# Weight words loaded one pair sooner and five weight conversions moved into the first batch's pairs

## The chip, the cores and the metric

The kernel runs on one core of a Trainium2 chip. The metric is the device time in microseconds (us), as the median of several runs. All times inside an execution are counted from the start of its span.

## The reference: what is computed

Feature-map attention over 8 batches of 8 heads, 576 tokens and head width 64, followed by a mixer over the 512 channels that the heads make together:

```python
def phi(x):
    proj = np.einsum('bhsd,df->bhsf', x, w_phi)
    proj = proj - np.max(np.abs(proj), axis=-1, keepdims=True)
    return np.concatenate([np.exp(proj), np.exp(-proj)], axis=-1)
q_p, k_p = phi(q), phi(k)
kv, z = np.einsum('bhsf,bhsd->bhfd', k_p, v), np.sum(k_p, axis=2)
x = np.einsum('bhsf,bhfd->bhsd', q_p, kv) / (np.einsum('bhsf,bhf->bhs', q_p, z)[..., None] + 1e-06)
# heads side by side: x is (8, 576, 512)
h = x.transpose(0, 2, 1) @ U @ V          # over tokens, rank 32
u = x + h.transpose(0, 2, 1)
out = u + np.maximum(u @ w_ch1, 0.0) @ w_ch2   # 512 -> 2048 -> 512
```

q, k, v and w_phi are float32. U, V and the two channel matrices are float64 and come to the chip as pairs of 32-bit words.

## The kernel before

**Work.** Attention goes in 32 pairs of heads, four to a batch: pair (b, j) is heads 2j and 2j+1 of batch b. For each pair k, q and v are loaded (`Pair`, `load_v`), k and q are transposed, projected (`pk`, `pq`), turned into features (`kp`, `qp`: absolute maxima, a subtraction, two exponentials on ACT, L372/L373 and L384/L385; for `qp` the maximum is an all-reduce on POOL, L382), the keys are summed with v on TensorE (`kv_ps`), and the outputs (`xp`, `xpt`) are divided and put into the token tile `x`. In batches 0 and 1 the transposes go through TensorE and PSUM, later through DVE. When all four pairs of a batch are there, `Tokens` mixes over tokens: `split` makes high and low parts `xs`, `down` multiplies by U into `pp` and then `pst`, `up` multiplies by V (`vp`) and adds. Then a `Mixer` tile transposes 512 tokens (`pt`, `uT_hi`, `uT_lo`) and runs 16 blocks of `hidden` (L651, 12 matmuls into `ph`; then `h_hi` on ACT and `h_lo` on DVE) and `add` (L672, 12 matmuls into four `o` tiles). The 64 last tokens of all batches make a ninth tile at the end.

**Weights.** The channel matrices come in 16 blocks. `load_weights(f)` issues two transfers of 512 KB on SP. `convert_block(i)` turns half a block into float32 parts: three ACT operations (L137, L138, L140), one shift on DVE (L141), an integer addition on POOL (L145), a copy (ACT for w1, DVE for w2, L239) and a subtraction on DVE (L240). There are 32 such conversions, here called blocks too where it is plain. Blocks 0 and 8 are also stored to memory (`kept`, L236) for later batches. Block 15's words use the place of `x0`, the first batch's tokens.

**Order.** A scheduler that plans with costs of its own sets the order on each engine from the order in which the code is traced; on the chip each engine then runs its list in that order. The code traces attention in steps (`step`), and after each step `Pace.step` adds other work: conversions up to a number that grows with the step count `steps[0]` (`blocks`), pieces of the first batch's token work (`pieces`), chunks of the mixer (`mix`), and, while the mixer has no chunks, one matmul over zeros (`keep_busy`), which is pinned in program order. A conversion is held behind the last operations put into `made` (the splits, `pst`, sums and transposed tiles of the first batch):

```python
for ins in made[-1:]:
    for i in ins:
        order.enter_context(tc.issue_after(i.ins))
convert_block(converted[0])
```

The words of blocks up to `LOADS[n]` are loaded at the start of pair number n, and held behind that pair's own loads.

**Names in the order's rows.** `qp0_2_1` is the query feature tile of pair (0,2), second half; `T1_0_3` the transposed q of pair (0,3) (T0 is k); `w1_0_ab` a working tile of the conversion of block 0 of w1; the number behind is a running number.

Of the kernel before, what the change touches and what calls it, by code (L numbers as in the profile page):

```python
# [25 lines left out]
def tile_kernel(  # L26
# [26 lines left out]
    NFC = DFF // P  # L53
# [135 lines left out]
    LAST = NFC - 1  # L189
# [523 lines left out]
    def weights(upto):  # L713

        while loaded[0] <= min(upto, LAST):
            load_weights(loaded[0])
            loaded[0] += 1
# [23 lines left out]
    steps = [0]  # L741

    class Pace:
# [5 lines left out]
        def step(self):  # L749

            steps[0] += 1
            upto = (steps[0] - CONVERT[0]) * 2 * NFC // (CONVERT[1] - CONVERT[0])
            if not pieces:
                blocks(upto)
            else:
                pieces.pop(0)()
                blocks(upto)
                if not pieces:
                    self.chunks, self.steps = 32 - HELD, BATCH - steps[0]
                else:  # L760
                    keep_busy(1, True)
                return
            n = (self.at + 1) * self.chunks // self.steps - self.at * self.chunks // self.steps
            self.at += 1
            mix(n)
            if not self.chunks:

                keep_busy(1, True)

# [9 lines left out]
            if here:  # L779
                tc.keep_in_program_order(ins)  # L780

    LOADS = (-1, 1, 4, 8, 12, LAST)
    CONVERT = (28, 63)
    BATCH = 67
    pieces = []
    HELD = 4
# [57 lines left out]
    def first_tokens(tk):  # L844
        m = []

        def begin():
            tk.up(2)
            tk.up(3)
            m.append(Mixer(tk.b, tk.x))  # L850
            m[0].transposes(0)

        def end():
            m[0].transposes(3)
            todo.extend(m[0].chunks())

        return [
            lambda: tk.split(1),
            lambda: [tk.down(1)] + [tk.up(t) for t in range(2)],
            lambda: [begin(), m[0].transposes(1), tk.up(NT)],  # L860
            lambda: [m[0].transposes(2), end()]]

    if True:
        cur = Pair(0, 0)
        load_w_phi()
        cur.load_v()
        nxt = Pair(0, 1)
        load_uv()
        nxt.load_v()
        keep_busy(6)  # L870
        cur.transposes()
        cur.s_project_k0()
        cur.s_project_k1()
        cur.s_project_q0()
        nxt.transposes()
        cur.s_kv()
        cur.s_project_q1()
        x = home.tile([P, NT, C], F32, tag="w_last", name="x0")
        xt = moe.tile([P, C], F32, tag="xt", name="xt0")
        nc.vector.memset(xt[ST:P], 0.0)  # L880
        tk = Tokens(0, x, xt)
        for n, (b, j) in enumerate(pairs):

            far = Pair(*pairs[n + 2]) if n + 2 < len(pairs) else None
            if far is not None:
                far.load_v()
            if n < len(LOADS):

                with tc.issue_after(far.loaded.ins):
                    weights(LOADS[n])  # L890
            if nxt is not None:
                step(nxt.s_project_k0)
            step(cur.s_out, x, xt)
            if nxt is not None:
                step(nxt.s_project_k1)
            pace.step()
            if j == 1:
                tk.split(0)
            if j == NPAIR - 1:
                fill = []  # L900
                if nxt is not None:
                    fill = [far.transposes, nxt.s_project_q0, nxt.s_kv, nxt.s_project_q1]
                if b == 0:
                    pieces.extend(first_tokens(tk))
                    pieces.pop(0)()
                    for fn in fill:
                        step(fn)
                else:
                    tokens(tk, fill)
                    pace = Pace(32 - HELD, 34)  # L910
                if nxt is not None:
                    if b % 2 == 1:
                        xt = moe.tile([P, C], F32, tag="xt", name=f"xt{b + 1}")
                        nc.vector.memset(xt[ST:P], 0.0)
                    x = moe.tile([P, NT, C], F32, tag="x", name=f"x{b + 1}")
                    tk = Tokens(b + 1, x, xt)
            else:
                if n == 0:
                    convert_uv()
                if far is not None:  # L920
                    step(far.transposes)
                if j == 1:
                    step(tk.down, 0)
                step(nxt.s_project_q0)
                step(nxt.s_kv)
                step(nxt.s_project_q1)
            cur, nxt = nxt, far
        mix(len(todo) - HELD)
        x = moe.tile([P, NT, C], F32, tag="x", name="x_tail")
        nc.sync.dma_start(out=x, in_=u_rows(B))  # L930
        m = Mixer(B, x)
        m.load_blocks()
        for c in range(NCC):
            m.turn_blocks(c)
            mix()
        todo.extend(m.chunks())
        mix(len(todo))
# [31 lines left out]
```

## Time and profile before

| | |
|---|---|
| median of 3 runs | 1175.15 us (1172.83 to 1176.64) |
| the profiled execution | 1178.5 us, span 1176.7 us |
| granted TensorE clock, mean | 0.989 |
| busy PE / DVE / ACT / POOL | 1133.4 / 671.2 / 542.1 / 204.3 us |
| matmuls over zeros | 37 |
| matmul groups of the mixer (L651 and L672) | 3456 matmuls of 128x512 |

PE is TensorE's matmuls, PEld its weight loads, DVE VectorE, ACT ScalarE, POOL GpSimd, SP the engine that issues the transfers. A timeline row gives start, length, engine, line, operation, tile written and tiles read, how many were merged, and in brackets the idle time ahead and what ended it. Lengths of neighbouring rows overlap a little, so the distance between two starts is the better price of one operation.

### The profile page before, as it was taken

What the parts mean: (1) busy time and instruction counts of PE and PEld (TensorE: products, weight loads), DVE (VectorE), ACT (ScalarE), POOL (GpSimd) and SP (SyncE); (2) the same over time, 40 slices, a digit from 0 to 9 for tenths busy, and PEclk for the clock granted to TensorE, in tenths of its full rate; (3) what the DMA queues carried; (4) which work ended last, traced back from release to release, by engine and by line L of the source; (5) the groups of instructions that cost most, each with busy time, mean ns of one, the idle gap of its engine ahead of it and who ended that gap; (6) DMA issues with size and microseconds to landing.
All of it is one profiled execution on the core that took longest, in us unless ns stands there. A gap on an engine that the chain in (4) does not pass through costs nothing.

```text
span 1176.7 us, 22653 instructions
## 1 busy us (share of the span) xinstructions
PE 1133.4 (96%) x8845; PEld 928.1 (79%) x8845; DVE 671.2 (57%) x1482; ACT 542.1 (46%) x1151; POOL 204.3 (17%) x154
## 2 busy tenths in 40 slices
PE   8998999999999999999999999999999999999998
PEld 6767877778877787778787887788777887888886
DVE  5567888766666656765656566765666543312111
ACT  6678887545443544454434554454544431111110
POOL 3334455211111111011111111111101110000000
PEclk8999999999999999999999999999999999999999
DMA  5775321431334223441344124522344026310101
GB/s 148 229 232 209 113 58 32 113 95 32 71 101 105 49 59 85 85 104 31 85 106 117 28 55 115 109 55 53 82 96 103 1 72 157 99 36 6 67 1 36
DMA packets 248427, 100.89 MB, mean 86 GB/s; under 512 B 215424, under 2 KB 227968, under 8 KB 248320
## 3 DMA queue, kind: packets, MB, share of 16 engines
q1 hardware_dynamic: 248000, 98.92, 32.8%
q8 instruction: 70, 1.15, 0.4%
q10 hardware_dynamic: 320, 0.52, 0.1%
q14 instruction: 37, 0.30, 0.1%
HBM read 78.41 MB, written 20.97 MB: 84 GB/s over the span
## 4 chain that ended last, share of the span: by engine, by line
PE 67%; DVE 11%; SPq 8%; DMA 7%; ACT 3%; issue 2%; POOL 1%; DVEq 0%; ACTq 0%; POOLq 0%
PE o L672 25%; PE ph L651 25%; SPq L279 5%; PE kv_ps L464 4%; PE xp L508 3%; SPq L637 2%; DMA raw<-in_k_dram 2%; DMA raw<-in_q_dram 2%; DVE T L338 2%; PE pp L587 2%; DVE raw L334 1%; PE pk L403 1%; PE pk L418 1%; DVE w L240 1%; PE kv_ps L455 1%
## 5 line engine op out<-in xcount | busy, mean ns | idle before, releaser
L651 PE MATMUL ph<-uT_hi,w 128*128 128x512 f32 x1152 | 387.2, 398 | 8.2 <-DVE den_t L478 3.6
L672 PE MATMUL o<-w,h_hi 128*128 128x512 f32 x1152 | 326.7, 398 | 7.5 <-ACT h_hi L656 7.5
L651 PEld LDWEIGHTS ph<-uT_hi,w 128*128 128x128 f32 x1152 | 217.5, 189 | 60.0 <-DVE h_lo L657 6.3
L672 PEld LDWEIGHTS o<-w,h_hi 128*128 128x128 f32 x1152 | 211.4, 189 | 52.3 <-ACT h_hi L656 12.1
L651 PE MATMUL ph<-uT_lo,w 128*128 128x512 f32 x576 | 227.0, 394 | 2.4 <-DVE uT_lo L249 2.4
L656 ACT ACTIVATE h_hi<-ph 128x512 fp32r<-128x512 f32 x144 | 85.6, 595 | 265.0 <-PE ph L651 253.6
L657 DVE SCALAR_TENSOR_TENSOR h_lo<-ph,h_hi 128x512 fp32r<-128x512 f32 x144 | 98.9, 687 | 170.9 <-ACT h_hi L656 170.0
L672 PE MATMUL o<-w,h_lo 128*128 128x512 f32 x576 | 192.7, 397 | 0.9 <-DVE h_lo L657 0.9
L382 POOL PARTITION_ALL_REDUCE qp<-qp x64 | 128.8, 2014 | 307.7 <-ACT qp L381 307.3
L651 PEld LDWEIGHTS ph<-uT_lo,w 128*128 128x128 f32 x576 | 109.4, 190 | 24.5 <-DVE uT_lo L249 2.9
L672 PEld LDWEIGHTS o<-w,h_lo 128*128 128x128 f32 x576 | 105.4, 188 | 22.1 <-DVE h_lo L657 2.1
L382 POOL PARTITION_ALL_REDUCE qp_t<-qp_t x32 | 26.2, 820 | 368.3 <-ACT qp_t L381 368.3
L334 DVE STREAM_TRANSPOSE raw<-raw 128x512 f32<-128x512 f32 x48 | 34.1, 711 | 92.5 <-DMA raw<-in_k_dram 39.4
L337 ACT CAST T<-raw 64x512 fp32r<-64x512 f32 x96 | 59.4, 618 | 51.0 <-PE pq L442 48.8
L372 ACT ACTIVATE kp<-kp 128x512 f32<-128x512 f32 x64 | 40.4, 631 | 92.0 <-DVE kp L369 91.9
L508 PEld LDWEIGHTS xp<-kv,qp 128*64 128x64 f32 x2048 | 66.4, 139 | 16.3 <-issue 7.8
L508 PE MATMUL xp<-kv,qp 128*64 128x65 f32 x2048 | 73.5, 226 | 5.3 <-ACT qp L384 4.0
L338 DVE TENSOR_TENSOR T<-raw,T 64x512 fp32r<-64x512 f32 x96 | 68.0, 708 | 17.6 <-ACT T L337 15.1
L464 PE MATMUL kv_ps<-vb,kp 128*64 128x65 f32 x2048 | 71.2, 224 | 0.0
L464 PEld LDWEIGHTS kv_ps<-vb,kp 128*64 128x64 f32 x2048 | 64.2, 137 | 8.6 <-issue 3.8
L384 ACT ACTIVATE qp<-qp 128x512 f32<-128x512 f32 x64 | 40.4, 631 | 65.8 <-DVE qp L383 65.8
L421 ACT COPY kp<-pk 128x256 f32<-128x256 f32 x96 | 34.0, 370 | 44.6 <-PE pk L418 43.7
(125 smaller groups left out, 1328.2 us busy)
## 6 DMA issues: line engine op xcount, KB each, us to landing
words<-in_moe_w_ch_dram SPq DMA_DIRECT2D x32, 512.0 KB, 7.2
w<-kept SPq DMA_DIRECT2D x30, 512.0 KB, 4.7
vb<-in_v_dram SPq DMA_DIRECT2D x64, 128.0 KB, 3.1
u_dram<-x SPq DMA_DIRECT2D x32, 256.0 KB, 2.1
st<-u_dram SPq DMA_DIRECT2D x16, 512.0 KB, 4.6
out_dram<-st SPq DMA_DIRECT2D x32, 256.0 KB, 2.5
y<-u_dram SPq DMA_DIRECT2D x112, 64.0 KB, 2.4
raw<-in_k_dram SPq DMA_DIRECT2D x192, 32.0 KB, 2.0
```

The costliest lines, as they stand in the source:

```text
L279: self.loaded = nc.sync.dma_start(out=m[i * Q:(i + 1) * Q, g, :].rearrange("c (j r) -> c j r", r=Q), in_=src[b, self.h0 + g, rs, cs].rearr ...
L334: nc.vector.transpose(out=x_, in_=x_)
L337: nc.scalar.copy(out=m[here, s, :], in_=x_[here])
L338: nc.vector.tensor_sub(m[there, s, :], x_[here], f32(m[here, s, :]))
L372: nc.scalar.activation(out=kp[:, :, 0:F], in_=kp[:, :, F:2 * F], func=AF.Exp)
L382: nc.gpsimd.partition_all_reduce(qp[:, 0, :], qp[:, 1, :], P, ReduceOp.absmax)
L464: nc.tensor.matmul(self.kv_v[r_, f, g, :], kp[:, t, f * F + i * H:f * F + (i + 1) * H], self.vb[:, g, t, :], start=False, stop=(t == NT - ...
L508: nc.tensor.matmul(xv[i * H:(i + 1) * H, c, :], qp[:, f, c * P + i * H:c * P + (i + 1) * H], self.kv[:, f, c // 2 if self.split else s, :] ...
L651: nc.tensor.matmul(ph, w1_part(f, l, c), r[:, c, :], start=(n == 0), stop=(n == 3 * NCC - 1))
L656: on_act = nc.scalar.activation(out=h_hi, in_=ph, func=AF.Relu)
L657: on_dve = nc.vector.scalar_tensor_tensor(out=h_lo, in0=ph, scalar=0.0, in1=f32(h_hi), op0=ALU.max, op1=ALU.subtract)
L672: ins = nc.tensor.matmul(self.o[t], l[:, cs], w2_t[f][:, r, :], start=(f == 0 and n == 0), stop=(f == NFC - 1 and n == 2))
```

## The change

Four edits. (1) `LOADS` loses its first entry, so that blocks 0 and 1 are loaded with pair 0 and each later group one pair sooner. (2) Conversions: before, the count was (step - 28) * 32 // 35, so the first came at step 30. Now it is (min(step, 26) - 10) * 5 // 16 up to step 30, which traces one at each of steps 14, 17, 20, 23 and 26, and 5 + (step - 31) * 27 // 32 from step 31, which gives the sixth at step 33. Both end at step 63. Steps 9 to 25 are those of pairs 1 and 2. (3) `Pace.step` leaves out its matmul over zeros at steps 8 to 22; in pair 0 three are added ahead of and three behind the outputs. (4) Two empty pieces follow the first batch's token work, so that the mixer's chunks begin two steps later: the first `hidden` is traced at step 36 for 34, behind the outputs of pair (1,0) instead of ahead of them.

```diff
@@ Pace.step
-            upto = (steps[0] - CONVERT[0]) * 2 * NFC // (CONVERT[1] - CONVERT[0])
+            if steps[0] < CONVERT[0]:
+                upto = (min(steps[0], EARLY[1]) - EARLY[0]) * EARLY[2] // (EARLY[1] - EARLY[0])
+            else:
+                upto = EARLY[2] + (steps[0] - CONVERT[0]) * (2 * NFC - EARLY[2]) // (
+                    CONVERT[1] - CONVERT[0])
...
-            if not self.chunks:
+            if not self.chunks and not 7 < steps[0] < 23:
 
                 keep_busy(1, True)
@@
-    LOADS = (-1, 1, 4, 8, 12, LAST)
-    CONVERT = (28, 63)
+    LOADS = (1, 4, 8, 12, LAST)
+    EARLY, CONVERT = (10, 26, 5), (31, 63)
@@ first_tokens
-            lambda: [m[0].transposes(2), end()]]
+            lambda: [m[0].transposes(2), end()],
+            lambda: None, lambda: None]
@@ the loop over pairs
+            if n == 0:
+                keep_busy(3, True)
             step(cur.s_out, x, xt)
+            if n == 0:
+                keep_busy(3, True)
```

What the scheduler makes of it, at three places. **First place: the end of batch 0's first token half, pairs 2 and 3.** ACT before, from the copy of the first `pst`:

```order
L590 CAST pst0_671<-pp0_0_672 128x256
L347 COPY T1_0_3_667<-T1_0_3_662 128x512
L381 COPY qp0_2_1_740<-pq1_0_2_737 128x512
L372 ACTIVATE kp0_3_t_773<-kp0_3_t_773 128x128
L373 ACTIVATE kp0_3_t_773<-kp0_3_t_773 128x128
L384 ACTIVATE qp0_2_0_690<-qp0_2_0_690 128x512
L381 COPY qp0_3_t_858<-pqt0_3_856 128x128
L385 ACTIVATE qp0_2_0_690<-qp0_2_0_690 128x512
```

ACT now, from the same copy of `pst` on; the rows go on in the next fence with the last of the twelve:

```order
L590 CAST pst0_679<-pp0_0_680 128x256
L137 ACTIVATE w1_0_ab_693<-words0_1_307 128x512
L138 ACTIVATE w1_0_ab_693<-words0_1_307 128x512
L140 ACTIVATE w1_0_ab_693<-words0_1_307 128x512
L137 ACTIVATE w2_0_ab_758<-words0_2_308 128x512
L138 ACTIVATE w2_0_ab_758<-words0_2_308 128x512
L140 ACTIVATE w2_0_ab_758<-words0_2_308 128x512
L137 ACTIVATE w1_1_ab_883<-words1_1_311 128x512
L138 ACTIVATE w1_1_ab_883<-words1_1_311 128x512
L140 ACTIVATE w1_1_ab_883<-words1_1_311 128x512
L137 ACTIVATE w2_1_ab_921<-words1_2_312 128x512
L138 ACTIVATE w2_1_ab_921<-words1_2_312 128x512
```

Four conversions stand between `pst` and the T1 copy of pair (0,3). ACT now, further on:

```order
L140 ACTIVATE w2_1_ab_921<-words1_2_312 128x512
L347 COPY T1_0_3_677<-T1_0_3_672 128x512
L381 COPY qp0_2_1_752<-pq1_0_2_749 128x512
L372 ACTIVATE kp0_3_t_796<-kp0_3_t_796 128x128
L381 COPY qp0_3_t_877<-pqt0_3_875 128x128
L239 CAST w1_0_699<-w1_0_ab_693 128x512
L357 COPY tail_T1_0_894<-tT1_0_892 64x2x64 x2
L384 ACTIVATE qp0_2_0_706<-qp0_2_0_706 128x512
L372 ACTIVATE kp0_3_0_805<-kp0_3_0_805 128x4x128
L239 CAST w1_1_889<-w1_1_ab_883 128x512
L137 ACTIVATE w1_2_ab_1026<-words2_1_545 128x512
```

Behind the last row come two more operations of that conversion, an exponential of `kp0_3_t`, and then the second exponential of `qp0_2_0` (L385). TensorE there, before:

```order
L446 MATMUL pq1_0_2_737<-T1_0_2_457,w_two_89 128x2x128 x2
L395 MATMUL pkt0_3_771<-w_f_87,tail_T0_3_651 128x128
L403 MATMUL pk0_0_3_779<-w_two_89,T0_0_3_658 128x256 x2
L778 LDWEIGHTS zeros_115
L778 MATMUL busy_685<-zeros_115 128x512
L433 MATMUL pqt0_3_856<-tail_T0_3_651,w_f_87 128x128
L493 MATMUL xpt0_2_790<-kv0_2_733,qp0_2_t_626 64x65 x4
L324 MATMUL tT1_0_868<-ident_82,t_r1_0_752 128x128
L342 MATMUL T0_1_0_872<-ident_82,raw1_0_0_748 128x128 x4
L778 LDWEIGHTS zeros_115
L778 MATMUL busy_696<-zeros_115 128x512
L508 MATMUL xp0_0_2_803<-kv0_2_733,qp0_2_0_690 64x65 x2
```

and now:

```order
L493 MATMUL xpt0_2_811<-kv0_2_747,qp0_2_t_640 64x65 x4
L433 MATMUL pqt0_3_875<-tail_T0_3_661,w_f_87 128x128
L324 MATMUL tT1_0_892<-ident_82,t_r1_0_772 128x128
L342 MATMUL T0_1_0_896<-ident_82,raw1_0_0_768 128x128 x4
L342 MATMUL T1_1_0_905<-ident_82,raw1_0_1_770 128x128 x4
L446 MATMUL pq0_0_3_912<-T1_0_3_677,w_two_89 128x2x128 x2
L782 LDWEIGHTS zeros_115
L782 MATMUL busy_930<-zeros_115 128x512
L508 MATMUL xp0_0_2_824<-kv0_2_747,qp0_2_0_706 64x65 x16
L508 MATMUL xp1_0_2_845<-kv0_2_747,qp0_2_1_752 64x65 x2
L403 MATMUL pk1_0_3_866<-w_two_89,T0_0_3_668 128x256 x2
```

The transposes of pair (1,0) and the projection of q of pair (0,3) now all stand ahead of the outputs of pair (0,2), and two zeros between them are gone.

**Second place: the second token half and the first mixer tile.** ACT before:

```order
L137 ACTIVATE w1_0_ab_1128<-words0_1_531 128x512
L138 ACTIVATE w1_0_ab_1128<-words0_1_531 128x512
L140 ACTIVATE w1_0_ab_1128<-words0_1_531 128x512
L381 COPY qp1_0_0_1143<-pq0_1_0_1140 128x512
L137 ACTIVATE w2_0_ab_1177<-words0_2_532 128x512
L138 ACTIVATE w2_0_ab_1177<-words0_2_532 128x512
L140 ACTIVATE w2_0_ab_1177<-words0_2_532 128x512
L590 CAST pst0_671<-pp0_1_1107 128x256
```

ACT now, from the split to the first transposed tile:

```order
L248 CAST xs0_1_4_1125<-xt0_296 128x256
L381 COPY qp1_0_0_1174<-pq0_1_0_1171 128x512
L590 CAST pst0_679<-pp0_1_1148 128x256
L248 CAST uT_hi0_1188<-pt0_0_1190 128x4x128
L384 ACTIVATE qp1_0_0_1174<-qp1_0_0_1174 128x512
L347 COPY T1_1_1_1146<-T1_1_1_1141 128x512
L381 COPY qp1_0_1_1266<-pq1_1_0_1263 128x512
```

The two conversions ahead of `pst` are gone. Behind the last `uT_hi` copy and two operations of block 2 of w2, ACT now goes on so (before, six conversion operations stood there, of blocks w1_1 and w2_1):

```order
L140 ACTIVATE w2_2_ab_1272<-words2_2_546 128x512
L137 ACTIVATE w1_3_ab_1323<-words3_1_549 128x512
L138 ACTIVATE w1_3_ab_1323<-words3_1_549 128x512
L372 ACTIVATE kp1_1_t_1308<-kp1_1_t_1308 128x128
L140 ACTIVATE w1_3_ab_1323<-words3_1_549 128x512
L137 ACTIVATE w2_3_ab_1387<-words3_2_550 128x512
L138 ACTIVATE w2_3_ab_1387<-words3_2_550 128x512
L140 ACTIVATE w2_3_ab_1387<-words3_2_550 128x512
L372 ACTIVATE kp1_1_0_1317<-kp1_1_0_1317 128x4x128
L373 ACTIVATE kp1_1_t_1308<-kp1_1_t_1308 128x128
L384 ACTIVATE qp1_0_1_1266<-qp1_0_1_1266 128x512
L656 ACTIVATE h_hi0_0_1409<-ph0_0_1396 128x512
```

Nine conversion operations are now ahead of the exponential of `qp1_0_1`.

**Third place: SP's queue ahead of pair (1,1).** Before:

```order
L217 DMA words4_2_768<-in_moe_w_ch2_dram 128x1024
L307 DMA vb0_91<-in_v_dram 128x4x64
L296 DMA t_r1_1_955<-in_k_dram 64x2x64
L285 DMA raw1_1_0_951<-in_k_dram 128x2x256
L296 DMA t_r1_1_955<-in_q_dram 64x2x64
L285 DMA raw1_1_1_953<-in_q_dram 128x2x256
```

and now:

```order
L214 DMA words8_791<-in_moe_w_ch1_dram 128x4x256
L217 DMA words8_791<-in_moe_w_ch2_dram 128x1024
L296 DMA t_r1_1_986<-in_k_dram 64x2x64
L296 DMA t_r1_1_986<-in_q_dram 64x2x64
L236 DMA kept0_104<-w2_0_764 128x1024
L285 DMA raw1_1_0_982<-in_k_dram 128x2x256
L236 DMA kept0_104<-w1_0_699 128x1024
L285 DMA raw1_1_1_984<-in_q_dram 128x2x256
```

The words of four more blocks and the two stores of block 0 now stand ahead of that pair's raw tiles.

## Prediction

> **What bounds the kernel now.** I read the page first, then busy time in windows cut at the stages, then the rows of each engine at the places where the order changes.
>
> ```profile
> span 1176.7 us, 22653 instructions
> ...
> PE 1133.4 (96%) x8845; PEld 928.1 (79%) x8845; DVE 671.2 (57%) x1482; ACT 542.1 (46%) x1151; POOL 204.3 (17%) x154
> ```
>
> ```profile
> 16.00:30.00 14.00, 11.18 (x124) 8.43 (x123) 12.26 (x40) 9.40 (x24) 7.12 (x7) 0.77 0.54 147
> ...
> 54.00:66.00 12.00, 11.91 (x159) 9.04 (x158) 5.78 (x18) 7.14 (x16) 5.08 (x5) 1.00 0.69 220
> ...
> 76.00:92.00 16.00, 11.93 (x153) 9.56 (x151) 11.76 (x25) 12.62 (x25) 6.58 (x4) 0.99 0.71 225
> ...
> 108.00:160.00 52.00, 52.00 (x412) 43.27 (x411) 39.49 (x72) 44.37 (x87) 28.09 (x21) 1.00 0.38 109
> 160.00:180.00 20.00, 17.37 (x129) 13.09 (x128) 17.73 (x37) 17.23 (x32) 6.82 (x5) 0.91 0.06 10
> 180.00:245.00 65.00, 60.00 (x503) 48.25 (x502) 51.96 (x106) 40.47 (x84) 20.05 (x13) 0.97 0.29 79
> 245.00:1000.00 755.00, 736.45 (x6056) 608.02 (x6055) 457.23 (x1035) 345.33 (x754) 109.44 (x69) 1.00 0.34 79
> ```
>
> The columns are the stretch, its length, busy PE, PEld, DVE, ACT and POOL, the granted TensorE clock, the DMA share and GB/s. From 245 on TensorE is busy 736.45 of 755 us and its work is fixed, so nothing changed earlier is absorbed there: the end moves by as much as the state at 245 moves. Everything the diff touches lies ahead of 245, and there TensorE loses time in few places: 2.8 of 14 us in the first pairs, 4.1 of 16 from 76 on, 2.6 of 20 from 160 on and 5.0 of 65 after that, plus half clock where the last but two columns fall under 1.00. I follow one number through the program: how much later (+) or earlier (-) than before the changed kernel is at a given instruction.
>
> **Matmuls over zeros.** 37 become 30: fifteen steps lose theirs, six are added in the first pair, two come with the empty pieces.
>
> ```profile
> L778 PE MATMUL busy<-zeros x37: 376/389/634, 1.2 to 85.6; 128*128 128x512 bf16 x37
> ...
> 49.02 0.39 PE L778 MATMUL busy<-zeros 128*128 128x512 bf16 x1
> 49.34 0.56 PE L464 MATMUL kv_ps<-vb,kp 128*64 128x65 f32 x10
> ```
>
> One costs the next matmul 0.32 us (49.02 to 49.34). By the order, up to the second transposes of pair 3 both kernels have nine of them behind 28 us, so the six new ones and those left out cancel: 0. The dip of the clock near 24 us (0.50 below) has its cause in a wait for an exponential, which stays; its bounds are -3.4 (it is gone: 6.8 us at half) and +1.3 (three zeros at half clock on the path), and I take -0.5, near nothing. From there to the last q projection of pair 2 three are gone, three times 0.32: -0.9, and the first pst copy, which two of them and a few matmuls of kv_ps precede, comes near 48.0.
>
> **The twelve conversion operations on ACT.** This is the step that decides. Five blocks are traced earlier, but all are held behind the first pst copy, and the order puts four of them, twelve ACT operations, in one piece right behind it, ahead of T1 of pair 3.
>
> ```profile
> 48.85 0.37 ACT L590 CAST pst<-pp 128x256 fp32r<-128x256 f32 x1 [1.83 <-PE pp L587]
> 51.00 0.59 ACT L347 COPY T<-T 128x512 f32<-128x512 f32 x1 [1.77 <-PE pq L446]
> 51.48 0.59 ACT L381 COPY qp<-pq 128x512 f32<-128x512 f32 x1
> ...
> 52.53 0.61 ACT L384 ACTIVATE qp<-qp 128x512 f32<-128x512 f32 x1
> ...
> 53.19 0.63 ACT L385 ACTIVATE qp<-qp 128x512 f32<-128x512 f32 x1
> ...
> 89.16 0.79 ACT L137 ACTIVATE w_ab<-words 128x512 uint16<-128x512 uint16 x1
> ...
> 92.77 0.63 ACT L372 ACTIVATE kp<-kp 128x512 f32<-128x512 f32 x1
> ```
>
> ```profile
> 54.78 1.04 PE L508 MATMUL xp<-kv,qp 128*64 128x65 f32 x28
> ...
> 57.73 1.13 PE L403 MATMUL pk<-w_two,T 128*128 128x256 f32 x4
> ...
> 72.71 1.04 PE L508 MATMUL xp<-kv,qp 128*64 128x65 f32 x28 [0.90 <-ACT qp L385]
> ```
>
> Six such operations ran from 89.16 to 92.77, 0.60 us each, so twelve hold ACT 7.2 us where it idled 1.77. With pst at 48.0 and 0.4 long they end at 55.6: the T1 copy is 4.6 late. Behind it stand a copy, an exponential, a copy, a cast and two short copies (2.6 us) before the first exponential of qp0_2_0, at 58.2 for 52.53; then an exponential, a cast, three more conversion operations and a short one (3.2 us, and the exponential's own 0.6) before the second, at 62.0 for 53.19. TensorE has work until about 52; its next transposes need the PSUM tile that the late qp copy frees, about 57, and the outputs of pair 2 need both exponentials. So it idles near 52 to 57 and near 60 to 62.6, outputs come at 62.6, and after 1.04 for them and 0.3 for two of the next half, pk (57.73 before) runs at 64.0: +6.3. Two fewer zeros until the next pair's keys: +5.7. DVE and POOL carry their parts of these blocks beside this wait, at no cost as long as ACT is the later one. Bounds: +2 (only the T1 copy counts) and +8.8 (the second exponential's delay in full).
>
> **What comes back before the mixer.** At the outputs of pair 3 the two exponentials now stand together, so the 0.90 wait at 72.71 goes, with one zero 0.3: +4.5.
>
> ```profile
> 76.02 1.41 PE L587 MATMUL pp<-xs,u_all 128*128 128x256 f32 x9
> ...
> 80.32 0.37 ACT L590 CAST pst<-pp 128x256 fp32r<-128x256 f32 x1
> ...
> 83.68 0.43 DVE L141 TENSOR_SCALAR w_ab<-w_ab 128x512 int32<-128x512 int32 x1
> ...
> 86.99 0.87 DVE L141 TENSOR_SCALAR w_ab<-w_ab 128x512 int32<-128x512 int32 x1
> ...
> 89.64 0.67 DVE L240 TENSOR_TENSOR w<-w_ab,w 128x512 fp32r<-128x512 f32 x1
> ```
>
> Before, six conversion operations kept the second pst copy until 80.32 though its matmuls ended at 77.43; the new order has none there: -2.8, to +1.7. Between pst and the last uT_lo DVE ran conversion work of about 1.7 us (three rows above, by their overlap with the next); gone too, less 0.3 for a zero that the empty pieces add: -1.4, to +0.3. Bounds of both together: 0 and -4.5.
>
> ```profile
> 23.90 0.49 PE L508 MATMUL xp<-kv,qp 128*64 128x65 f32 x4 [1.74 <-ACT qp L384]
> ...
> 89.32 0.49 PE L651 MATMUL ph<-uT_hi,w 128*128 128x512 f32 x1 [0.68 <-ACT uT_hi L248]
> 92.22 0.80 PE L651 MATMUL ph<-uT_lo,w 128*128 128x512 f32 x1 [2.40 <-DVE uT_lo L249]
> ...
> 96.30 0.34 PE L508 MATMUL xp<-kv,qp 128*64 128x65 f32 x4
> ...
> 108.10 2.72 PE ph L651 x12
> ```
>
> ```profile
> 24.00:25.00 1.00, 1.00 (x6) 0.79 (x7) 0.65 (x2) 0.51 (x1) 1.00 (x3) 0.50 0.63 141
> ...
> 90.00:91.00 1.00, 0.00 (x0) 0.00 (x0) 1.00 (x4) 1.00 (x3) 0.00 (x0) 1.00 1.03 410
> ...
> 92.00:93.00 1.00, 0.78 (x2) 0.69 (x3) 0.92 (x5) 1.00 (x3) 0.00 (x0) 0.50 1.10 402
> ```
>
> The first hidden tile waited 0.68 and 2.40 us and then ran at half clock: 4.1 us from 92.22 to 96.30 for eleven matmuls, which take 2.5 at 2.72 for twelve. In the new order keys and outputs of pair (1,0) stand right ahead of it, so the wait is filled and the clock should hold: -1.5, to -1.2. Then nine conversion operations (5.4 us) and three exponentials follow the last uT_hi copy (about 90.4) on ACT, ahead of the exponential that the next outputs need: those come at 97.9 for 96.30: +1.6 instead of -1.2.
>
> The clock: after waits of 0.68 and 2.40 us with one matmul between them it is at 0.50 at 92, and after a wait of 1.74 us it is so at 24. [...]
>
> **The order of transfers.** Words wait less, but raw tiles of pair (1,1) now stand behind two stores of converted weights (ready about 57 and 59).
>
> ```profile
> DMA to landing us min/median/max: 2.8/3.1/8.7
> ...
> 69.50 0.60 PE L342 MATMUL T<-ident,raw 128*128 128x128 f32 x4
> ```
>
> Issued at 60 they land by 68.7 at the slowest; their transposes, at 69.50 before, come near 74: hidden, 0, with 5 us to spare. If that cover went it would cost what exceeds it.
>
> **The stage with the conversions.** Both kernels have 27 or 28 blocks to run until step 63, the new one some two blocks ahead at the same hidden tile.
>
> ```profile
> 163.08 0.78 ACT L137 ACTIVATE w_ab<-words 128x512 uint16<-128x512 uint16 x1
> ...
> 168.79 0.61 ACT L384 ACTIVATE qp<-qp 128x512 f32<-128x512 f32 x1
> ...
> 169.45 0.34 PE L508 MATMUL xp<-kv,qp 128*64 128x65 f32 x4 [1.44 <-ACT qp L384]
> ```
>
> Nine operations in front of an exponential, and TensorE waited: the idle 2.6 us from 160 to 180 with clock 0.91 (1.8 us lost) are the price of such a place, 4.4. The new order has six there instead of nine, but another nine a little earlier. Bounds: +4.4 (one more such place) and -11.4 (all idle and half clock from 160 to 245: 2.6, 5.0, 1.8 and 0.03 of 65). I take -3.3, three quarters of the one place, since it is the nearest row.
>
> **Sum.** -0.5 + 1.6 - 3.3 = -2.2. The profiled execution took 1178.5 us, 3.3 over the median 1175.15, so 1176.3 in its own time and 1173.0 as a median: a gain within 0.3% (3.5 us), which is about what runs of this kernel can tell from no change.
>
> **Rivals.** *Slower.* The piece of twelve is not won back: its place is ACT from 48 to 62, its price +5.7, and it decides if the first uT_lo matmul (92.22 before) comes after 95. For it speaks that DVE runs 11.76 of 16 us from 76 to 92 and may pace that chain without ACT; against it, the 2.8 us at pst are ACT's alone. Then only those 2.8 and the 1.2 return: 5.7 - 1.2 - 2.8 = +1.7 at the mixer, +1.6 + 1.2 for the nine operations behind it, no gain later, -0.5: +4.0 to +5, a median near 1180.
>
> *Faster.* The crowded stage gains more: the place at 163 goes in full (-4.4) and half of the rest up to 245 (5.0 + 1.9, half 3.5) with it: -0.5 + 1.6 - 7.9 = -6.8, and 1168.3; with the dip near 24 gone, 1165.4. For it: ACT is busy 44.37 of 52 us from 108 on, so each block done sooner helps; against it: TensorE was never idle there.
>
> *No effect.* The twelve operations cost what the later ones give back and the stage to 245 lines up as before: 1175. It lies in the same class as the forecast.
>
> [...]
>
> **How the numbers follow.** 0.42 for the forecast's class (no effect and the clock's rule in it), 0.36 for faster, 0.22 for slower: the late gain has the longer reach, the early loss the firmer mechanism. The likeliest alone spans 1171.6 to 1178.7. Leaving out about one in ten at each end, the range is 1165 to 1180.
>
> **What would show it.** The profile after should show twelve conversion operations in a row on ACT near 48 to 56, TensorE idle near 52 to 57 for an ACT copy, no conversion between the split and the second pst copy, the first hidden tile without the 2.40 wait and within 1 us of 92, outputs of pair (1,0) waiting for ACT near 96, and less idle time than 2.6 and 5.0 us in 160 to 180 and 180 to 245. The prediction is wrong if the twelve are spread out or hidden, if the first hidden tile comes after 95 or ahead of 89, or if the stage after 108 shifts by more than 5.

## The result, and the profile after

The changed kernel takes 1186.17 us (median of 4 runs, 1184.27 to 1190.74); the kernel before, beside it, 1175.21 us (1172.83 to 1176.64). The ratio is 1.0101, 95% interval 1.0067 to 1.0135: slower by about 11 us, outside the predicted range of 1165 to 1180. The profiled execution is the longest of the four (1190.74 us, 4.6 over its median), so sizes are read below from it and from a second execution of the same program.

Span and busy times of the page after:

```profile
span 1189.0 us, 22620 instructions
...
PE 1134.1 (95%) x8833; PEld 929.1 (78%) x8838; DVE 671.5 (56%) x1482; ACT 542.4 (46%) x1151; POOL 205.3 (17%) x154
```

TensorE is as busy as before (1133.4). What was added is idle time and half clock, and the windows of the prediction say where (after, same columns):

```profile
54.00:66.00 12.00, 7.00 (x52) 5.60 (x54) 9.27 (x17) 10.44 (x24) 8.11 (x6) 0.65 1.03 366
...
108.00:160.00 52.00, 49.21 (x362) 40.20 (x364) 31.55 (x64) 38.07 (x77) 19.03 (x15) 1.00 0.14 29
160.00:180.00 20.00, 17.98 (x154) 14.76 (x148) 18.58 (x32) 16.78 (x32) 13.13 (x8) 0.91 0.22 68
180.00:245.00 65.00, 60.16 (x463) 48.70 (x464) 51.13 (x102) 42.22 (x85) 20.20 (x13) 0.95 0.27 69
245.00:1000.00 755.00, 732.71 (x6088) 603.69 (x6089) 458.64 (x1045) 345.00 (x754) 109.89 (x69) 0.99 0.33 77
```

From 54 to 66 TensorE is busy 7.00 of 12 us at clock 0.65 (before 11.91 at 1.00). From 108 to 160, where it was never idle, 2.8 us are now missing, and 180 to 245 is no better than it was.

**The front.** ACT after, from the first of the twelve to the second exponential of `qp0_2_0`:

```profile
48.12 0.79 ACT L137 ACTIVATE w_ab<-words 128x512 uint16<-128x512 uint16 x1
...
54.78 0.64 ACT L140 ACTIVATE w_ab<-words 128x512 f32<-128x512 f32 x1
55.32 0.56 ACT L347 COPY T<-T 128x512 f32<-128x512 f32 x1
...
57.69 0.63 ACT L384 ACTIVATE qp<-qp 128x512 f32<-128x512 f32 x1
...
61.27 0.62 ACT L385 ACTIVATE qp<-qp 128x512 f32<-128x512 f32 x1
```

TensorE after, at the same place and behind the first hidden tile:

```profile
56.41 1.97 PE L342 MATMUL T<-ident,raw 128*128 128x128 f32 x8 [5.12 <-ACT qp L381]
...
61.94 1.04 PE L508 MATMUL xp<-kv,qp 128*64 128x65 f32 x28 [1.02 <-ACT qp L385]
64.19 0.34 PE L508 MATMUL xp<-kv,qp 128*64 128x65 f32 x4 [1.21 <-ACT qp L384]
64.46 2.04 PE L403 MATMUL pk<-w_two,T 128*128 128x256 f32 x4
...
94.42 0.50 PE L651 MATMUL ph<-uT_hi,w 128*128 128x512 f32 x1
94.76 0.48 PE L651 MATMUL ph<-uT_lo,w 128*128 128x512 f32 x1
...
100.21 0.34 PE L508 MATMUL xp<-kv,qp 128*64 128x65 f32 x4 [2.67 <-ACT qp L384]
```

The row of twelve is there, the wait of 5.12 for the late `qp` copy, and `pk` at 64.46 (57.73 before). `pk` runs 2.04 us for 1.13: half clock (0.50 from 64.52 to 67.94), on the path. The outputs behind the first hidden tile come at 100.21 for 96.30, 3.9 late.

**The mixer's stage.** TensorE before, at the second token half of batch 1 and at the start of the second mixer tile:

```profile
144.33 1.35 PE L587 MATMUL pp<-xs,u_all 128*128 128x256 f32 x10
145.51 2.00 PE L672 MATMUL o<-w,h_hi 128*128 128x512 f32 x8
...
150.99 1.07 PE L672 MATMUL o<-w,h_lo 128*128 128x512 f32 x4
151.89 0.61 PE L455 MATMUL kv_ps<-vt,kp_t 128*128 128x130 f32 x4
...
235.90 0.49 PE L651 MATMUL ph<-uT_hi,w 128*128 128x512 f32 x1 [0.72 <-ACT uT_hi L248]
237.62 0.45 PE L493 MATMUL xpt<-kv,qp_t 128*64 128x65 f32 x8 [1.23 <-DVE kp L422]
```

TensorE after, at the same places:

```profile
152.15 1.36 PE L587 MATMUL pp<-xs,u_all 128*128 128x256 f32 x10
153.34 1.03 PE L446 MATMUL pq<-T,w_two 128*128 128x256 f32 x4
154.02 0.58 PE L651 MATMUL ph<-uT_lo,w 128*128 128x512 f32 x1
...
155.37 1.08 PE L672 MATMUL o<-w,h_lo 128*128 128x512 f32 x4
158.75 0.71 PE L455 MATMUL kv_ps<-vt,kp_t 128*128 128x130 f32 x4 [2.30 <-DVE pst L591]
...
180.18 1.66 PE L403 MATMUL pk<-w_two,T 128*128 128x256 f32 x4 [2.20 <-DVE xt L483]
...
238.90 1.25 PE L623 MATMUL pt<-ident,x 128*128 128x128 f32 x8 [0.84 <-DVE st L693]
...
242.01 1.52 PE L418 MATMUL pk<-w_hl,T 128*128 128x256 f32 x4 [0.69 <-DVE xt L606]
244.73 0.80 PE L651 MATMUL ph<-uT_lo,w 128*128 128x512 f32 x1 [1.20 <-DVE uT_lo L249]
```

Between `pp` and `kv_ps` stand nine matmuls of the mixer (L651 and L672; before, 24), and then 2.30 us of nothing until DVE has finished `pst`. The chain that TensorE waits for grew by 0.6 us only: from the end of `pp` to the end of `pst` on DVE it took 4.6 us before and takes 5.2 now, and in both six conversion operations stand ahead of the `pst` copy on ACT (about 3 us of it). What changed more is the work that covers it. At the second tile three waits add to 2.7 us (before, two of 0.72 and 1.23). Half clock follows both (after, 157 to 167 and 238 to 248):

```profile
157.00:167.00 10.00, 8.26 (x86) 7.24 (x87) 9.75 (x15) 10.00 (x19) 6.65 (x4) 0.83 0.45 137
238.00:248.00 10.00, 7.01 (x24) 4.92 (x24) 9.68 (x19) 4.38 (x9) 0.00 (x0) 0.70 0.51 145
```

### The profile page after: what moved, and what is told of

It reads as the page before. It is cut to its first block, busy times and chain, and to the rows that moved or that the text cites. A ratio compares the mean times of both kernels' runs of the same rounds, so it can differ in the third digit from the quotient of the medians.

```text
span 1189.0 us, 22620 instructions
## 1 busy us (share of the span) xinstructions
PE 1134.1 (95%) x8833; PEld 929.1 (78%) x8838; DVE 671.5 (56%) x1482; ACT 542.4 (46%) x1151; POOL 205.3 (17%) x154
## 4 chain that ended last, share of the span: by engine, by line
PE 64%; DVE 15%; SPq 8%; DMA 7%; issue 2%; ACT 2%; POOL 1%; DVEq 0%; ACTq 0%; POOLq 0%
PE ph L651 24%; PE o L672 23%; SPq L279 5%; PE kv_ps L464 4%; PE xp L508 3%; SPq L637 3%; DVE T L338 2%; DMA raw<-in_k_dram 2%; DMA raw<-in_q_dram 2%; PE pp L587 2%; DVE raw L334 1%; DVE w L240 1%; PE pk L403 1%; DVE qp L383 1%; DVE uT_lo L249 1%
## 5 line engine op out<-in xcount | busy, mean ns | idle before, releaser
L651 PE MATMUL ph<-uT_hi,w 128*128 128x512 f32 x1152 | 386.3, 397 | 8.6 <-DVE den_t L478 4.9
L672 PE MATMUL o<-w,h_hi 128*128 128x512 f32 x1152 | 327.9, 398 | 6.0 <-ACT h_hi L656 6.0
L651 PEld LDWEIGHTS ph<-uT_hi,w 128*128 128x128 f32 x1152 | 217.0, 189 | 59.5 <-DVE h_lo L657 6.4
L672 PEld LDWEIGHTS o<-w,h_hi 128*128 128x128 f32 x1152 | 211.6, 189 | 50.4 <-ACT h_hi L656 9.5
L651 PE MATMUL ph<-uT_lo,w 128*128 128x512 f32 x576 | 226.1, 392 | 1.2 <-DVE uT_lo L249 1.2
L656 ACT ACTIVATE h_hi<-ph 128x512 fp32r<-128x512 f32 x144 | 85.7, 595 | 271.0 <-PE ph L651 259.8
L672 PE MATMUL o<-w,h_lo 128*128 128x512 f32 x576 | 194.8, 398 | 2.2 <-DVE h_lo L657 2.2
L651 PEld LDWEIGHTS ph<-uT_lo,w 128*128 128x128 f32 x576 | 109.2, 190 | 23.5 <-DVE uT_lo L249 1.7
L672 PEld LDWEIGHTS o<-w,h_lo 128*128 128x128 f32 x576 | 104.9, 188 | 23.7 <-DVE h_lo L657 4.3
```

The lines of the kernel that those rows point to most:

```text
L651: nc.tensor.matmul(ph, w1_part(f, l, c), r[:, c, :], start=(n == 0), stop=(n == 3 * NCC - 1))
L656: on_act = nc.scalar.activation(out=h_hi, in_=ph, func=AF.Relu)
L672: ins = nc.tensor.matmul(self.o[t], l[:, cs], w2_t[f][:, r, :], start=(f == 0 and n == 0), stop=(f == NFC - 1 and n == 2))
```

## The experiments

Offsets below are ends of `h_hi` (L656) against the profile before: the first, the 25th (the second tile's ninth, at 307.20 before, behind the stage) and the last. The start rows of the first and the 25th, before and after:

```profile
96.41 0.60 ACT L656 ACTIVATE h_hi<-ph 128x512 fp32r<-128x512 f32 x1 [0.43 <-PE ph L651]
...
306.60 0.60 ACT L656 ACTIVATE h_hi<-ph 128x512 fp32r<-128x512 f32 x1
```

```profile
100.02 0.62 ACT L656 ACTIVATE h_hi<-ph 128x512 fp32r<-128x512 f32 x1
...
314.20 0.58 ACT L656 ACTIVATE h_hi<-ph 128x512 fp32r<-128x512 f32 x1
```

Ratios are to the kernel before on the same chip (its median was 1174.9 to 1179.4 us from chip to chip, so times of different groups are not compared). The offsets are of one execution each, against one profile of the kernel before that is itself 3.3 us over its median; the ratios decide. "Cover" is the number of mixer matmuls that the order puts between `pp` of batch 1's second half and the next `kv_ps`, "wait" TensorE's there.

| run | ratio (95%) | first | 25th | last | cover | wait |
|---|---|---|---|---|---|---|
| changed kernel | 1.0101 (1.0067 to 1.0135) | +3.6 | +7.6 | +12.3 | 9 | 2.30 |
| the same again | 1.0084 (1.0053 to 1.0115) | +5.7 | +10.0 | +10.9 | 9 | 2.45 |
| no early conversion | 0.9986 (0.9966 to 1.0005) | +1.3 | -4.2 | -5.0 | 24 | none |
| words and early alone | 1.0091 (1.0067 to 1.0116) | +5.6 | +6.8 | +11.0 | 16 | 0.79 |
| unheld | 1.0093 (1.0062 to 1.0125) | +1.1 | +9.4 | +9.8 | 9 | 2.58 |
| same pace | 1.0002 (0.9986 to 1.0018) | +1.7 | -1.8 | -1.8 | 17 | none |
| same pace, unheld | 0.9968 (0.9947 to 0.9989) | -0.1 | -6.2 | -6.4 | 17 | none |
| two early | 1.0035 (1.0022 to 1.0047) | -2.8 | +4.2 | +0.1 | 24 | none |
| ahead, none early | 1.0019 (1.0000 to 1.0038) | +2.1 | +0.2 | +2.1 | 14 | 0.65 |
| BATCH 66 | 1.0057 (1.0035 to 1.0078) | +5.3 | +5.9 | +7.7 | 9 | 2.45 |
| BATCH 68 | 1.0054 (1.0032 to 1.0077) | +6.2 | +8.0 | +6.0 | 14 | 1.03 |
| two early, same pace | 1.0000 (0.9981 to 1.0019) | -0.7 | -1.8 | +2.4 | 16 | 0.28 (ACT) |
| none early, BATCH 63 | 0.9945 (0.9927 to 0.9962) | +0.8 | -8.7 | -9.8 | 24 | none |
| before, BATCH 63 | 1.0009 (0.9994 to 1.0025) | -1.7 | -2.0 | +0.2 | 24 | none |
| same pace, unheld, 63 | 0.9931 (0.9913 to 0.9949) | +0.6 | -8.0 | -8.4 | 24 | none |
| front alone | 1.0010 (0.9993 to 1.0026) | +4.7 | -0.1 | -0.8 | 24 | none |
| unheld, BATCH 66 | 0.9999 (0.9978 to 1.0019) | +3.0 | +1.4 | -1.0 | 6 | 1.58 (ACT) |

**Which edit.** The first theory was that the twelve operations start the loss. *No early conversion:*

```diff
-    EARLY, CONVERT = (10, 26, 5), (31, 63)
+    EARLY, CONVERT = (10, 26, 0), (28, 63)
```

> The changed kernel with its second edit undone: no conversion before step 30, the other three edits kept. Theory (the twelve conversion operations behind the first pst copy start the loss): no such row on ACT, the keys' projection behind pair 2's outputs (64.46 in the changed kernel, 57.73 before) at 56.5 to 58, the first h_hi within 1.5 us of the kernel before, and a median of 1172 to 1178. Rival A (the missing zeros or the empty pieces cost it): 1183 to 1189. Rival B (the stage from 108 to 245 loses its time whatever comes ahead of it): first h_hi as before, but 4 us or more late at 245, and 1179 to 1183.

1175.56 us, beside 1177.86 of the kernel before: the loss is gone. *Words and early conversions alone* (zeros and pieces as before):

> The kernel before with earlier words and the five early conversions alone (edits 1 and 2; zeros and pieces as before). Theory: the twelve stand in one row again, the keys' projection behind pair 2's outputs near 64 to 65, the first h_hi 3 to 5 us late, and a median of 1182 to 1188. Rival A (zeros or empty pieces): 1173 to 1177. Rival B: 1179 to 1184 with at most 2 us of it at the first h_hi.

1188.90 us, a little over the expected range: they carry all of it, and the zeros and empty pieces none. *Unheld:*

```diff
-                for ins in made[-1:]:
+                for ins in made[-1:] if steps[0] > 26 else []:
```

> The changed kernel with the five early conversions no longer held behind the last pst copy. The order puts nine of the twelve operations ahead of the first pst copy (three, an exponential or copy between, six) and three behind it. Theory: what they delay is then the pst copy, which TensorE needs only for the tokens' second step, so the exponentials of pair 2's queries are 2 to 4 us late instead of 6 to 8, the keys' projection at 59 to 62, the first h_hi -1 to +2 us, and a median of 1175 to 1182. Rival A: 1183 to 1189, as the changed kernel. Rival B: first h_hi at +1 or less and 1179 to 1184.

This broke the first theory. The front was mended as foreseen (first `h_hi` +1.1 for +3.6 and more), yet the time stayed: 1188.26 us, with 8 us lost from the first to the 25th `h_hi`. *The same kernel again:*

> The changed kernel as it is, for a second profile. Its first profile ran 4.6 us over the median, and its offset to the kernel before grew from about +8 at 245 to +12.3 at the end. If that growth lies in the order of the instructions, the offset grows by 3 to 5 us from 245 to the end again; if it belongs to that one execution, the offset at the end is within 1.5 us of that at 245. The first h_hi at +3 to +4.5 in both cases, median 1184 to 1189.

1188.90 us. From the 25th `h_hi` on this execution loses 0.9 us where the first lost 4.7, so that growth belongs to the execution, not to the order. The front's size varies too (+5.7 for +3.6).

**The new theory: the later pace.** With five conversions done, the count from step 31 runs ahead of the one before; in the order that the scheduler makes of it, the mixer's matmuls stand further forward, out of the places where they covered waits of batch 1. *Same pace* keeps the five and then takes the count before; the second run adds the unheld line:

```diff
-                upto = EARLY[2] + (steps[0] - CONVERT[0]) * (2 * NFC - EARLY[2]) // (
-                    CONVERT[1] - CONVERT[0])
+                upto = max(EARLY[2], (steps[0] - 28) * 2 * NFC // (CONVERT[1] - 28))
```

> The changed kernel with the five early conversions, but from step 31 on the count of the kernel before (five until it passes five). The twelve stand behind the first pst copy as in the changed kernel; on TensorE the order stands from the second pst of batch 1 on as in the run without early conversions: 17 mixer matmuls between pp of batch 1 and the next kv_ps (9 in the changed kernel, 24 before) and 22 and 14 ahead of the transposes of the second mixer tile (8 and 0 in the changed kernel). Theory (most of the loss is mixer matmuls run too soon, so that fewer are left to cover the waits of batch 1's tokens and the second tile): first h_hi at +3 to +6 as in the changed kernel, no wait over 1 us on pst near 157, no half clock from 235 to 250, and a median of 1176 to 1182. Rival E (the twelve operations alone carry the loss): 1185 to 1189.

> The last kernel with the five early conversions not held behind pst: nine operations ahead of the first pst copy, three behind it. Theory: first h_hi at 0 to +2, the stage behind it as in the last kernel, and a median of 1173 to 1179. Rival E: 1178 to 1183 (nine operations in place of twelve). Rival F (early conversions lose in the mixer's stage whatever the order, by the stores of converted weights or by the transfers): 1184 to 1189, as the run that was only unheld.

1176.84 and 1172.78 us (kernel before 1174.91): as the theory had it, the second a little faster still. Its one clear miss is the front of the first, +1.7: the new count also left only three of the nine operations ahead of the next exponential. The two unheld kernels differ in the later count alone, by 15.6 us at the 25th `h_hi` and by 1.0093 against 0.9968 in the ratio, so the later count is shown to be a cause. *Two early* (`(10, 26, 2)`) and *ahead* (`(10, 26, 0), (26, 61)`: no early conversion, but the later ones ahead as in the changed kernel):

> The changed kernel with two early conversions for five: six operations in a row behind the first pst copy, and 30 conversions over steps 31 to 63. On TensorE 24 mixer matmuls stand between pp of batch 1 and kv_ps, but only 2 and 4 ahead of the second tile's transposes. Theory: first h_hi at +1 to +3, no wait on pst near 157, but waits of 2 us or more in all and half clock from 235 to 250: 1179 to 1185. Rival E, in proportion to the operations: half of the changed kernel's loss, 1180 to 1183, with nothing lost from 235 to 250.

> No early conversion, but the later ones by (step - 26) * 32 // 35: one or two ahead of the kernel before, as the changed kernel is from step 36 on. Six operations stand behind the first pst copy, 14 mixer matmuls between pp of batch 1 and kv_ps, 22 and 14 ahead of the second tile's transposes. Theory: a wait of 1.0 to 1.5 us on pst near 155, none of the half clock at the second tile, first h_hi at 0 to +2, 1174 to 1180. Rival G (being ahead with conversions in the mixer's stage is itself the loss): 1183 to 1189.

1180.30 and 1178.13 us. Two early conversions gain at the front, where a loss was expected, and lose 7 us in the stage, though not with the half clock at the second tile that was expected (clock 1.00 from 235 to 255; three waits from 233 to 240, 3.2 us in all): waits of 2.39 us at 201, with a clock of 0.57 from 200 to 208, and of 2.81 us at 264 are larger. Being ahead is not by itself the loss; without the early conversions it also left more cover (14 matmuls at `kv_ps`, 22 and 14 at the second tile).

**Is it the cover?** Two runs change only the mixer's pace in the changed kernel, `BATCH = 66` and `68` for 67:

> The changed kernel with one number of the mixer's pace changed, BATCH = 66 for 67; conversions, words, zeros and pieces as in the changed kernel. The order is the same up to 9 mixer matmuls between pp of batch 1 and kv_ps, but ahead of the second tile's transposes now stand 16 and 12 mixer matmuls (as in the kernel before; 8 and 0 in the changed kernel). Theory (the cover): first h_hi late by 3 to 6, the wait on pst near 157 again 2.0 to 2.7, but the second tile without a window of 10 us under a clock of 0.8, and a median of 1179 to 1185. Rival E (the early conversions carry the loss): 1185 to 1190.

> The changed kernel with BATCH = 68, the twelve behind the first pst copy kept. The order has 14 mixer matmuls between pp of batch 1 and kv_ps, 22 and 14 ahead of the second tile's transposes. Theory: first h_hi late by 3 to 6, a wait on pst of 1.0 to 1.5, the second tile as in the run without early conversions, and a median of 1177 to 1183. Rival E: 1185 to 1190.

1185.25 and 1184.76 us beside 1179.43. The waits on `pst` came as the cover says (2.45 with nine matmuls, 1.03 with fourteen). Between the first and the 25th `h_hi` these kernels lose 0.7 and 1.7 us, where the changed kernel lost 3.9 and 4.3; the fronts stay late (+5.3 and +6.2). By the ratios 3 to 5 us of the loss went, with intervals that overlap the changed kernel's: the times lie at the border between theory and rival, and don't tell them apart. *Two early, same pace* and the reverse, *none early, BATCH 63*:

> The changed kernel with two early conversions and then the count of the kernel before. The front is as in the run with two early conversions (first h_hi 2.75 us ahead of the kernel before there), 16 mixer matmuls between pp of batch 1 and kv_ps, 22 and 14 ahead of the second tile's transposes. Theory: first h_hi at -1 to -3.5, a wait on pst of at most 1, the second tile as without early conversions: 1166 to 1173, the fastest so far. Rival I (what the front gains is absorbed by the mixer's stage): 1173 to 1177.

> The reverse: no early conversion at all, conversions by the count of the kernel before, but BATCH = 63. The order has 24 mixer matmuls between pp of batch 1 and kv_ps as without early conversions, but 8, 4 and 0 ahead of the second tile's transposes, as in the changed kernel. Theory: first h_hi within 2 us of the kernel before, no wait on pst, and idle time and half clock from 235 to 250 as in the changed kernel: 1178 to 1183. Rival E (no early conversions, no loss): 1172 to 1177.

Both missed. The first stays at the time before, since its front lost what it had gained to a wait of 4.28 us on ACT at 95. The second has the changed kernel's little cover at the second tile and pays there (waits of 0.85, 0.69 and 1.49 us), and is 0.55% faster all the same: its mixer matmuls went to 150 to 200, where TensorE is busy 48.72 of 50 us (45.66 before, 45.50 after). So little cover at one wait need not be a loss: it can be paid for by cover at others, and the count at one place does not tell the time of the stage.

**The shares.** *Front alone* has the changed kernel's order to the first `h_hi`, the row of twelve and the nine included, and then the count before:

```diff
+                upto = EARLY[2] + (min(steps[0], FRONT) - CONVERT[0]) * (2 * NFC - EARLY[2]) // (
+                    CONVERT[1] - CONVERT[0])
+                upto = max(upto, (steps[0] - 28) * 2 * NFC // (CONVERT[1] - 28))
...
+    FRONT = 37
```

> The changed kernel with its conversions up to step 37 as they are (the twelve behind pst and the nine ahead of the exponential both stay), and from there the count of the kernel before as soon as it is larger. The order is the changed kernel's to the first h_hi, and then the one of the run without early conversions: 24 mixer matmuls between pp of batch 1 and kv_ps, 22 and 14 ahead of the second tile's transposes. Theory (both places count, the front 4 to 5 us, the stage the rest): first h_hi at +3.5 to +6.2, 10 us or less of idle time and half clock from 100 to 300 (14 to 19 in the changed kernel), and a ratio of 0.999 to 1.004. Rival K (the front carries all): 1.007 to 1.011.

1178.83 us beside 1177.97. TensorE of this run at the place of the 2.30 us:

```profile
144.36 1.35 PE L587 MATMUL pp<-xs,u_all 128*128 128x256 f32 x10
145.55 2.00 PE L672 MATMUL o<-w,h_hi 128*128 128x512 f32 x8
...
151.02 1.07 PE L672 MATMUL o<-w,h_lo 128*128 128x512 f32 x4
151.93 0.61 PE L455 MATMUL kv_ps<-vt,kp_t 128*128 128x130 f32 x4
```

Eight, twelve (in the rows left out) and four mixer matmuls now stand between `pp` and `kv_ps`, and no wait is left. With a front as late as the changed kernel's (+4.7) this kernel is level at the 25th `h_hi`; the changed kernel goes on to +7.6 and +10.0. Without its early conversions' effect on the later order the change would have cost nothing that can be measured.

That does not make the late front free. The run without early conversions has the same cover in the stage, and beside it this one is 3.5 us later at the first `h_hi`, 4.1 at the 25th and 4.2 at the end (ratios 1.0010 and 0.9986, with intervals that overlap): the front's loss lasts. That this kernel is still level with the one before comes from the stage, where both runs gain some 5 us on the one profile before. By the ratios, 11 to 14 us lie between the run without early conversions and the changed kernel; about 3 of them go to the front and 9 to 11 to the later order.

Last, *unheld with BATCH 66*, and `BATCH = 63` on the kernel before and on the fastest run with early conversions:

> The run that was only unheld (ratio 1.0093, first h_hi at +1.1, 6 to 9 us lost from 235 to 280), with BATCH = 66: 6 mixer matmuls between pp of batch 1 and kv_ps (9 there), 22 and 14 ahead of the second tile's transposes (8 and 0 there). Theory (what the stage loses is the number of mixer matmuls at each wait): a wait of 2.7 to 3.3 us on pst (4.4 less six times 0.23), at most 3 us lost from 235 to 280, and a ratio of 1.001 to 1.005. Rival F (early conversions lose in the stage whatever the order): 1.007 to 1.011.

> The kernel before with BATCH = 63 for 67 alone. Theory (the pace of the mixer decides how its matmuls are spread over the waits of batch 1, and 63 spreads them better wherever the conversions are): h_hi number 12 at least 5 us ahead of the kernel before, idle time and half clock from 100 to 300 together under 10 us (11.9 before), and a ratio of 0.993 to 0.998. Rival J (the gain needs the missing zeros and empty pieces, which the reverse run had): 0.998 to 1.003.

> Five early conversions, not held, the later count of the kernel before, and BATCH = 63. Theory: the gains of the two runs that it joins (0.9968 and 0.9945, both with about 7.5 us of idle time and half clock from 100 to 300) are largely the same time, so they do not add: 0.992 to 0.997. Rival: they add, 0.987 to 0.992.

Unheld, the one number BATCH takes the ratio from 1.0093 to 0.9999 and the part from the first to the 25th `h_hi` from +8.3 to -1.6, with cover back at the second tile, though the wait that I priced for it came otherwise (1.58 us, for ACT). This is the best support for the cover as the mechanism: the count that traces the conversions is the same in both. On the kernel before, 63 gains nothing (1.0009), so the gain of 63 needs the other edits; which of them was not tried. The last, 1169.52 us beside 1177.97, is the fastest: five early conversions not held, the later count before, a mixer paced to end by step 63. Its ratio of 0.9931 (0.9913 to 0.9949) is below both kernels'; it is not told apart from 0.9945 without early conversions.

## Why the prediction was wrong

**Zeros and the first pst copy: right, with some luck.** It starts at 47.85 (48.0 predicted), but at 49.26 in the second execution, so a microsecond and more of this belongs to the execution. The dip of the clock near 24, a term of -0.5, shrank in both (3.4 us at half clock for 6.8) without a gain that both show.

**The twelve operations: right in mechanism and nearly in size.** Exponentials at 57.69 and 61.27 (58.2 and 62.0), idle from 51.3 to 56.4 and near 61 to 62, `pk` at 64.46 (64.0).

**Left out: the half clock behind them.** The sum has no term for it, since I took TensorE to wait for ACT there anyway. For the half clock right behind the wait of 5.12 (0.50 from 54.28 to 61.11) that held, since another wait for ACT followed. But from 64 to 68, behind two shorter waits (1.02 and 1.21 us), TensorE was busy and the clock low again:

```profile
64.00:68.00 4.00, 3.81 (x26) 3.16 (x28) 2.76 (x7) 2.29 (x6) 1.27 (x1) 0.57 0.61 231
```

That is 3.81 times 0.43, 1.6 us on the path. The term belonged in the sum: with it, the outputs of pair (0,3) were 6.7 late (79.42 for 72.71), not 4.5. The "clock's rule" that the prediction names beside its chance of 0.42 is shown by no run; what this run showed in its place is the clock of 0.57 over these 4 us.

**What comes back before the mixer: right as differences.** 2.8 of it at the second pst copy (84.19 for 80.32, +3.9) and 1.3 at the first `uT_lo` matmul (94.76 for 92.22, +2.5); predicted 2.8 and 1.4. The wait ahead of the first hidden tile went, its eleven matmuls took 2.8 us for 4.1, and the nine operations cost as much as thought (+1.4 from +2.5 to +3.9; predicted +1.3). The front missed by 2.3 us in all (+3.9 for +1.6), most of it that window; in the second execution it is 2 us worse again, 1.4 of them already at the first pst copy.

**The stage with the conversions: this step failed.** I took -3.3; the runs show +3.9 and +4.3 from the first to the 25th `h_hi`. The place that I priced did go: no exponential makes TensorE wait from 160 to 180. But I did not ask what would be late next there. In its place stand 2.30 us on `pst` and 2.20 on the outputs' last step (`xt`, at 180), and at the second tile 2.7 us for 1.95, with half clock. I looked at conversion operations ahead of exponentials, and not at the number of mixer matmuls between one attention step and the next, which the same order told: 9 for 24, and 8, 4 and 0 ahead of the second tile's three groups of transposes for 16, 0 and 12. That this later order costs the time is shown (same pace, front alone, unheld with BATCH 66); the waits follow the count at `pst` (but for one run) and at the second tile. How much of the stage's time these waits carry stays open, since *none early, BATCH 63* has the second tile's waits and is fast. The upper bound of that term, +4.4, did hold the value.

**"From 245 on nothing is absorbed": right on average, wrong for one execution.** The offset changed by 4.7 and 0.9 us behind the 25th `h_hi` in two executions of one program, and by -4.1 to +4.3 in the other runs (+0.5 on average over all).

**The rivals.** "Slower" had the price at the outputs nearly right (+4 to +5; +3.9). Its condition, the first `uT_lo` matmul after 95, was missed in one execution (94.76) and met in the other (96.80); what decided was the stage behind it, where it forecast no gain and had no loss either. The weights of 0.36 for faster and 0.22 for slower followed from the sign of that one term.

## What to carry to other kernels

When work is traced earlier, ask not only what stands behind it but what the scheduler then moves forward: count the independent matmuls left at each later wait, in the new order, and price a wait by the chain it covers less that count times one matmul. The independent matmuls are a fixed number, so cover that one place gains another may lose; sum the whole stage. To separate a front from what follows, keep the order of the one and restore the other; both halves of this change were worth several microseconds, and that run told their shares apart.

## What the runs showed of the hardware

The same wait was followed by half clock in one execution and not in another. On `kv_ps`, the changed kernel waited 2.30 us and then ran at 0.83 on average over 10 us (above); the same program waited 2.45 us there and kept full clock:

```profile
160.93 0.71 PE L455 MATMUL kv_ps<-vt,kp_t 128*128 128x130 f32 x4 [2.45 <-DVE pst L591]
```

```profile
159.00:169.00 10.00, 8.07 (x93) 7.02 (x94) 9.60 (x14) 10.00 (x19) 6.68 (x4) 1.00 0.41 130
```

0.83 over 10 us is half clock for 3.4 us (0.50 from 160.10 to 163.51), a price of 1.7 us by my estimate from these numbers, since TensorE was busy all through. In the first profile after, the granted clock changes at 23.57, 26.98, 54.28, 61.11, 64.52, 67.94, 160.10, 163.51, 180.58, 183.99 us and so on, and in the profile before at 23.49, 30.32, 91.76, 95.17, 170.26, 173.68 and so on: in each, the distances are whole multiples of 3.41 us, and half clock lasts one or two of them. The first wait left TensorE 1.35 us of work in the stretch of that grid from 156.69 to 160.10, and the clock was 0.50 in the next one. In the second execution the clock falls at 183.14 (0.57 from 183 to 184). Counted back from there in steps of 3.41 us the grid lies at 155.84, 159.25 and 162.66, and it cut the wait in two: 2.65 us of work from 155.84 to 159.25 and 1.73 from 159.25 to 162.66, and the clock stayed at 1.00. In the profile before and the first one after, 13 stretches at full clock had 1.50 us of work or less, and the clock was 0.50 behind every one; it stayed at 1.00 behind every one with more than 2.4 us. Between the two either came: it stayed behind 1.63 us (before, from 450.16) and fell behind 2.17 (after, from 238.61).

Whether half clock followed a wait of 2.30 or 2.45 us thus went with where on the grid it fell. Between 54 and 71 us the changed kernel ran 10.2 us at half clock in the first execution and 13.7 in the second. That can have made at most some 0.6 of the 2 us by which their fronts differed, since 1.4 stood already at the first pst copy; the cause of those stays open.

The wait on `pst` followed the cover: 2.30 to 2.58 us with 9 mixer matmuls, 0.65 and 1.03 with 14, 0.79 or none with 16, none with 17 and 24. At 0.227 us for one matmul (2.72 us for twelve), matmuls and wait together come to 3.8 to 4.6 us where there was a wait. The one run with 6 does not fit: there TensorE waited 1.58 us for ACT, and not for `pst`.
